# Where the split sums of the dense weights are made, in an attention, mixture and dense-mixture kernel on one core

## The chip, the cores and the metric

The kernel is one program on one core of a Trainium2 chip. The number that counts is the device time of one execution in microseconds; it was run three times, and the median is given. One more execution was recorded by the hardware profiler, and everything that is read from a trace comes from that one.

## The reference

Three stages follow each other. Attention with pooled keys and values gives a matrix x of 4608 tokens by 512. A mixture of 8 experts changes the tokens whose skip score is positive, and a dense layer, called the dense mixture here, ends it.

```python
def reference(**kwargs):
    ...
    x = attention(q, k, v).transpose(0, 2, 1, 3).reshape(4608, 512)
    x = moe(x, w_skip, w_gate, w1, w2)   # one expert of 8 per token:
                                         # x + gate * (relu(x @ w1[e]) @ w2[e])
    h = x @ w_in                         # 512 -> 2048
    return np.maximum(0.01 * h, h) @ w_out   # 2048 -> 512
```

All of it is float32. The kernel gets float32 accuracy out of the matrix engine by splitting each operand into a high and a low half and adding three products: low by high, high by low, high by high.

## The kernel before, in words

**Stages.** Attention runs until about 243 us, the mixture of experts (the first mixture) until about 650 us, the dense mixture from there to the end.

**Engines.** PE is the matrix engine (TensorE), DVE is VectorE, ACT is ScalarE, POOL is GpSimd, and SP issues the transfers. In the first mixture and in the dense mixture PE, DVE, ACT and POOL run in the order in which the program is written. SP's order is set by a scheduler that knows the dependencies.

**The first mixture** takes the experts in the order `TURNS`, in units of at most four tiles of 128 tokens: expert r0 in two units of 4, r6 in one of 2, r1 in two (3 and 2), r7 in one of 1, r2 in two (3 and 2), r3, r4 and r5 in one of 3 each. For a unit, `turn` transposes and splits the gathered tokens, `up` makes one of 8 blocks of the hidden layer, `down` makes one tile of the result and scatters it back to `xd`. An expert has eight loads of raw weights of 512 KB, four of w1 (`split1`) and four of w2 (`split2`): `weight_load` puts one in a buffer `wraw`, `weight_split` makes its high half on ACT (L144) and its low half on DVE (L145), in three rings of pairs. The next expert's w1 is asked for at the last `up` and in the downs of an expert's last unit.

**The dense weights** come as pairs of 32-bit words, 1024 words for 512 values, in 32 halves. `convert` is called in two of eight `up` steps from the second unit on and behind each `down`. It loads one half (`cvraw`), makes two parts of it on ACT (L853, L854), joins them by four operations on DVE (L839 to L842) and adds the rest on POOL (L844) into `cvt`.

Then `finish` takes it on in the first mixture. The up-projection of the dense mixture is a product of 2 by 2 blocks in seven products instead of eight, so it needs four sums of blocks of `w_in`, `ta` and `tb` (DVE, L805 to L808), beside three blocks as they are. Sums and blocks are split (ACT L792, L812, L819; POOL L793, L813, L820) and stored as pairs in `wsd`, the halves of `w_out` in `wod` (L783). The work of one half is spread over four calls of `convert`.

**The dense mixture** takes 768 tokens at a time, six times, in 8 passes p over the hidden layer, so n = 8 s + p runs from 0 to 47. `up2(n)` makes the seven products (42 matmuls, four banks `pu`), puts them together on DVE (`add`, `leaky`) and splits the four results (`pair`: ACT, then POOL). `down2(n)` makes six tiles of 6 matmuls in four banks `pd`, and adds each to `y` (DVE L1213, or on ACT L1211 at p = 0). The program runs `up2(n)` ahead of `down2(n - 1)`. Between the two stand `ws_load(n + 2)`, which loads the pairs of `wsd`, and for p = 3, 4, 5 two `turn_x`, which transpose two tiles of the next 768 tokens into two banks `pd` and copy them on ACT (L1127). The four sums of x that the seven products need (`sums_x`, L1130 to L1133) stand there at p = 6, and its splits (`split_x`, L1137 and L1138) stand between the tiles of the down at p = 7. For the first 768 tokens the turns, sums and splits stand ahead of `up2(0)`.

Of the kernel before, what the change touches and what calls it, by code (L numbers as in the profile page):

```python
# [20 lines left out]
P = 128  # L21
# [9 lines left out]
E = 8  # L31
# [15 lines left out]
RINGS = (4, 4, 3)  # L47
# [7 lines left out]
def kernel(  # L55
# [61 lines left out]
    lst = dram.tile([E * CAP, 1], F32, name="lst")  # L117

# [660 lines left out]
    stages = [[], [], [], []]  # L779
    first_half = {}  # L780

    def pair_out(dst, hi, lo):
        stages[3].append(lambda: (nc.sync.dma_start(out=dst(0), in_=hi.bitcast(F32)), nc.sync.dma_start(out=dst(1), in_=lo.bitcast(F32))))  # L783

    def quarters(t):
        return t.rearrange("p (c q f) -> p q c f", c=2, q=2)

    def finish(cvp, j, h, t, size, low):

        b = j // 2  # L790
        if j % 2:
            nc.scalar.copy(out=low.bitcast(F32R), in_=t)  # L792
            nc.gpsimd.tensor_tensor(out=t.bitcast(F32R), in0=t, in1=low, op=ALU.subtract)  # L793
            pair_out(lambda i: wod[b, :, i, h * 512:(h + 1) * 512], low.bitcast(F32R), t.bitcast(F32R))
            return
        if h == 0:
            first_half[b] = t
            src, m, at = quarters(t)[:, 0:1], 256, 1024
        else:
            src, m, at = quarters(t), 512, 1280  # L800
            q0, q1 = quarters(first_half.pop(b)), src
            ta = cvp.tile([P, 2, 2, P], F32, tag="tf", name=f"ta{b}", bufs=3)
# [4 lines left out]
            V.tensor_tensor(out=ta[:, 1], in0=q1[:, 1], in1=ta[:, 0], op=ALU.subtract)
            V.tensor_tensor(out=tb[:, 1], in0=q1[:, 0], in1=ta[:, 1], op=ALU.subtract)  # L808
            for i, x in enumerate((ta, tb)):
                def sums(i=i, x=x.rearrange("p a c f -> p (a c f)")):  # L810
                    th = cvp.tile([P, 512], F32R, tag="th", name=f"th{b}_{i}", bufs=2)
                    nc.scalar.copy(out=th, in_=x)  # L812
                    nc.gpsimd.tensor_tensor(out=x.bitcast(F32R), in0=x, in1=th.bitcast(F32), op=ALU.subtract)  # L813
                    pair_out(lambda k: wsd[b, :, k, i * 512:(i + 1) * 512], th, x.bitcast(F32R))
                stages[2].append(sums)
        sh = dict(q=m // 256, c=2)
        hi = low[:, :m].bitcast(F32R)
        lo = size[:, :m].bitcast(F32R)
        nc.scalar.copy(out=hi.rearrange("p (q c f) -> p q c f", **sh), in_=src)  # L819
        nc.gpsimd.tensor_tensor(  # L820
            out=lo.rearrange("p (q c f) -> p q c f", **sh), in0=src,
            in1=low[:, :m].rearrange("p (q c f) -> p q c f", **sh), op=ALU.subtract,
        )
        pair_out(lambda i: wsd[b, :, i, at:at + m], hi, lo)

    def convert(cvp):

        for f in [stages[3].pop(0) for _ in range(len(stages[3]))]:
            f()
        for f in [stages[2].pop(0) for _ in range(len(stages[2]))]:  # L830
            f()
        if stages[1]:
            finish(cvp, *stages[1].pop(0))
        if stages[0]:
            j, h, hw, size, low = stages[0].pop(0)
            t = cvp.tile([P, 512], F32, tag="cvt", name=f"cvt{j}_{h}", bufs=3)
# [8 lines left out]
            stages[1].append((j, h, t, size, low))  # L845
        if halves:
# [4 lines left out]
            size = cvp.tile([P, 512], F32, tag="cvs", name=f"cvs{j}_{h}", bufs=4)  # L851
            low = cvp.tile([P, 512], F32, tag="cvl", name=f"cvl{j}_{h}", bufs=4)
# [25 lines left out]
    def ws_load(n):  # L878
        if n < 8 * NSB:
            ws[n] = dense_tiles(rings[1], f"ws{n}", wsd[n % 8], (1024, 768))  # L880

    def wo_load(n):
        if n < 8 * NSB:
            wo[n] = dense_tiles(rings[0], f"wo{n}", wod[n % 8], (1024,))[0]

    with ExitStack() as bctx:
# [4 lines left out]
        state["raws"] = bctx.enter_context(tc.tile_pool(name="raws", bufs=3))  # L891
        NXG = 8
# [97 lines left out]
        for u, (r, t0, n) in enumerate(UNITS):  # L990
# [4 lines left out]
            for f in range(8):  # L995
                up(u, f)
                if last:
                    if f < 4:
                        split2(r, f)
                    elif f == 4:  # L1000
                        ws_load(0)
# [4 lines left out]
                if f == 7 and t0 + n == TILES[r] and not last:  # L1006
                    split1(TURNS[k + 1], 0)
# [3 lines left out]
            if t0 + n == TILES[r] and not last:  # L1011
                todo = [lambda c=c: split1(TURNS[k + 1], c) for c in range(1, 4)]
# [281 lines left out]
```

## Time and profile before

| | us |
|---|---|
| median of three runs (lowest, highest) | 1454.66 (1452.83, 1455.26) |
| the profiled execution | 1452.53 |
| its span in the trace | 1450.7 |
| PE busy | 1345.0 (93% of the span) |
| DVE busy | 994.1 (69%) |
| POOL busy | 529.8 (37%) |
| ACT busy | 465.0 (32%) |

The span runs from the first to the last instruction on the core. The busy time of an engine is the time in which one of its instructions runs. A matmul's time depends on the granted clock, of which a profile gives the mean over a stretch as a share of full speed.

### The profile page before, as it was taken

The page shows a single profiled execution, that of the slowest core. Times are in us where ns is not written, and L with a number is a line of the kernel's source. Part 1 is how long each engine was busy: PE and PEld are TensorE (multiplying, and loading weights), DVE is VectorE, ACT ScalarE, POOL GpSimd, SP SyncE. Part 2 cuts the span into 40 slices and gives each one's busy share as a digit, 9 for nine tenths or more (in the row PEclk, how much of TensorE's full clock was granted, in tenths as well). Part 3 has the DMA queues.
Part 4 walks back from the last instruction along what each step waited for, and adds up shares of the span by engine and source line. Part 5 has one row for each costly group of instructions (what it writes and reads, how often), then busy time and mean ns, then how long its engine had stood idle before and what let it go on. Part 6 is the DMA issues. An engine that isn't in the chain of part 4 may idle for free.

```text
span 1450.7 us, 22090 instructions
## 1 busy us (share of the span) xinstructions
PE 1345.0 (93%) x8296; PEld 1201.4 (83%) x8296; DVE 994.1 (69%) x1647; ACT 465.0 (32%) x800; POOL 529.8 (37%) x458
## 2 busy tenths in 40 slices
PE   4888997998899799996999999999999999999998
PEld 4777886887788689985888988899899989988997
DVE  8676686368898785435668666856766686678565
ACT  2544542353545443323212221222231222213211
POOL 5983002047466372213324332332242233225222
PEclk7899998999897999997999999999999999999999
DMA  9994127357888866564654665556565655547541
GB/s 176 288 286 124 46 79 215 114 188 255 266 275 282 275 220 185 173 239 167 206 208 163 229 210 203 195 197 219 187 215 200 208 192 207 184 160 246 171 156 44
DMA packets 119926, 284.84 MB, mean 196 GB/s; under 512 B 12422, under 2 KB 40070, under 8 KB 119426
## 3 DMA queue, kind: packets, MB, share of 16 engines
q1 hardware_dynamic: 115010, 268.57, 57.5%
q0 software_dynamic: 4800, 14.77, 3.0%
q8 instruction: 67, 1.10, 0.3%
q14 instruction: 49, 0.40, 0.1%
HBM read 234.44 MB, written 49.94 MB: 196 GB/s over the span
## 4 chain that ended last, share of the span: by engine, by line
PE 67%; DVE 13%; DMA 9%; issue 5%; ACT 3%; POOL 2%; SPq 0%; POOLq 0%; DVEq 0%; ACTq 0%
PE d L1207 9%; PE d L1209 8%; PE d L1208 8%; PE u L1154 8%; PE u L1156 8%; PE u L1155 8%; DMA xd<-xg,idx 3%; PE sc L356 2%; DMA cvraw<-in_moe_w_out_dram 2%; PE bank L969 2%; PE pv L407 2%; PE bank L970 2%; PE bank L968 2%; PE bank L952 2%; PE bank L953 2%
## 5 line engine op out<-in xcount | busy, mean ns | idle before, releaser
L1175 POOL TENSOR_TENSOR gl<-g,gh 128x384 fp32r<-128x384 f32 x192 | 210.7, 1107 | 508.2 <-ACT gh L1173 503.8
L1207 PE MATMUL d<-wo_0whi,gl 128*128 128x512 f32 x576 | 226.3, 393 | 12.9 <-DVE y L1213 12.9
L1213 DVE TENSOR_TENSOR y<-d,y 128x512 f32<-128x512 f32 x252 | 168.9, 687 | 91.9 <-PE d L1209 90.8
L1209 PE MATMUL d<-wo_0whi,gh 128*128 128x512 f32 x576 | 225.0, 391 | 0.0
L1208 PE MATMUL d<-wo_0wlo,gh 128*128 128x512 f32 x576 | 224.8, 390 | 0.0
L1173 ACT CAST gh<-g 128x384 fp32r<-128x384 f32 x192 | 98.7, 514 | 307.3 <-DVE g L1169 307.3
L1162 DVE TENSOR_TENSOR g<-u,gp 128x384 f32<-128x384 f32 x144 | 79.8, 554 | 122.4 <-PE u L1156 115.1
L1169 DVE SCALAR_TENSOR_TENSOR g<-g 128x384 f32<-128x384 f32 x192 | 141.2, 735 | 5.0
L1207 PEld LDWEIGHTS d<-wo_0whi,gl 128*128 128x128 f32 x576 | 108.1, 188 | 37.9 <-DVE y L1213 15.0
L1154 PE MATMUL u<-more_h,ws_0wlo 128*128 128x384 f32 x384 | 129.3, 337 | 2.4 <-ACT more_h L1137 1.5
L1155 PE MATMUL u<-more_l,ws_0whi 128*128 128x384 f32 x384 | 129.1, 336 | 1.3 <-DVE more_l L1138 1.3
L1156 PE MATMUL u<-more_h,ws_0whi 128*128 128x384 f32 x384 | 129.0, 336 | 0.0
L953 PE MATMUL bank<-xl,whi 128*128 128x384 f32 (+3 forms) x352 | 120.8, 343 | 7.6 <-DVE xl L942 7.6
L1209 PEld LDWEIGHTS d<-wo_0whi,gh 128*128 128x128 f32 x576 | 108.1, 188 | 23.0
L1208 PEld LDWEIGHTS d<-wo_0wlo,gh 128*128 128x128 f32 x576 | 108.2, 188 | 21.0
L952 PE MATMUL bank<-xh,wlo 128*128 128x384 f32 (+3 forms) x352 | 120.2, 342 | 2.8 <-ACT xh L941 2.7
L954 PE MATMUL bank<-xh,whi 128*128 128x384 f32 (+3 forms) x352 | 120.0, 341 | 0.0
L969 PE MATMUL bank<-wlo,hh 128*128 128x512 f32 x240 | 97.2, 405 | 9.6 <-DVE wlo L145 9.6
L1179 ACT COPY gp<-u 128x384 f32<-128x384 f32 x48 | 23.0, 478 | 258.0 <-PE u L1156 258.0
L976 POOL DMA_INDIRECT xd<-xg,idx x30 | 41.4, 1381 | 171.0 <-DVE xg L972 170.3
L968 PE MATMUL bank<-whi,hl 128*128 128x512 f32 x240 | 97.3, 405 | 5.7 <-ACT whi L144 3.2
L970 PE MATMUL bank<-whi,hh 128*128 128x512 f32 x240 | 96.3, 401 | 0.0
(264 smaller groups left out, 2808.8 us busy)
## 6 DMA issues: line engine op xcount, KB each, us to landing
wraw<-in_moe_w_dram SPq DMA_DIRECT2D x64, 512.0 KB
ws_0whi<-wsd SPq DMA_DIRECT2D x48, 512.0 KB
ws_0wlo<-wsd SPq DMA_DIRECT2D x48, 512.0 KB
wo_0whi<-wod SPq DMA_DIRECT2D x48, 512.0 KB
wo_0wlo<-wod SPq DMA_DIRECT2D x48, 512.0 KB
ws_1whi<-wsd SPq DMA_DIRECT2D x48, 384.0 KB
ws_1wlo<-wsd SPq DMA_DIRECT2D x48, 384.0 KB
xr<-xd SPq DMA_DIRECT2D x36, 256.0 KB
```

The lines of the kernel that those rows point to most:

```text
L952: nc.tensor.matmul(ps, wl[:, c, fs], xh[:, c, :m], start=(c == 0), stop=False)
L953: nc.tensor.matmul(ps, wh[:, c, fs], xl[:, c, :m], start=False, stop=False)
L968: nc.tensor.matmul(ps, hl[:, f, ts_], wh[:, f % 2, :], start=(f == 0), stop=False)
L1154: nc.tensor.matmul(ps, wl[:, c], h[:, c], start=(c == 0), stop=False)
L1155: nc.tensor.matmul(ps, wh[:, c], l[:, c], start=False, stop=False)
L1156: nc.tensor.matmul(ps, wh[:, c], h[:, c], start=False, stop=(c == 1))
L1169: V.scalar_tensor_tensor(out=g[nm], in0=g[nm], scalar=0.01, in1=g[nm], op0=ALU.mult, op1=ALU.max)
L1175: G_.tensor_tensor(out=lo, in0=g[nm], in1=hi.bitcast(F32), op=ALU.subtract)
L1207: nc.tensor.matmul(ps, lo[:, ts_], wh[:, i], start=(i == 0), stop=False)
L1208: nc.tensor.matmul(ps, hi[:, ts_], wl[:, i], start=False, stop=False)
L1209: nc.tensor.matmul(ps, hi[:, ts_], wh[:, i], start=False, stop=(i == 1))
L1213: V.tensor_tensor(out=ys[t], in0=ps, in1=ys[t], op=ALU.add)
```

## The change

`convert` now only converts. Each half, once joined, is stored as it is in a new array `wd` (one store of 256 KB in the place of two pair stores or more), and the sums and splits are made when the dense mixture first needs a block. For n < 8, `ws_load(n)` is `ws_sums(n)` and `ws_blocks(n)`: a load of the whole block `draw` (512 KB), four sums on DVE, their high half on ACT and low half on POOL (1024 columns), and the same for the three blocks (768 columns in two pieces). The pairs are kept in the rings for the pass and stored to `wsd` for the five later ones. `wo_load(n)` does the same for `w_out`, with its low half on DVE. What the first pass loaded in pairs is now loaded once unsplit and stored in pairs. The blocks ws 0, wo 0, wo 1 and the sums of ws 1 are made in the first mixture's last unit, the three blocks of ws 1, wo 2 and wo 3 at the dense start.

Besides: the third ring has four pairs instead of three, the first mixture has a fourth raw buffer and ten gather buffers instead of eight; the raw buffers live through all stages; the next expert's w1 is asked for in the downs of an expert's first unit; in the dense mixture the four sums of x stand one by one behind tiles of the down at p = 6; the splits of x change engines; the six turns ahead of `up2(0)` alternate between ACT and DVE; and for n = 0 the fifth product is issued two places earlier.

In the first mixture this is ACT's row of instructions around the conversion of half 6, in the third unit, before (whi: an expert weight's high half; th, cvl: high halves of dense weights; cvs, cvl at L853 and L854: the conversion's parts; xh: a unit's tokens):

```order
L144 CAST whi_4255<-wraw_4253 128x1024
L812 CAST th_0_4261<-ta_4131 128x512
L812 CAST th_1_4264<-tb_4132 128x512
L792 CAST cvl_0_4058<-cvt_0_4139 128x512
L853 ACTIVATE cvs_0_4276<-cvraw_0_4274 128x512
L854 ACTIVATE cvl_0_4277<-cvraw_0_4274 128x512
L941 CAST xh<-bank_3220 128x4x128
```

And the same place now:

```order
L146 CAST whi_4189<-wraw_4187 128x1024
L807 ACTIVATE cvs_0_4201<-cvraw_0_4199 128x512
L808 ACTIVATE cvl_0_4202<-cvraw_0_4199 128x512
L951 CAST xh<-bank_3226 128x4x128
L951 CAST xh<-bank_3227 128x4x128
```

The three splits of dense weights between the expert weight and the conversion are gone.

On DVE, this is the start of the dense mixture before, up to the first addition of `up2(0)` (xl, more_l: low halves of x and its sums; s: the sums; xf<-tp: a turn's copy; g: an addition):

```order
L1138 TENSOR_TENSOR xl<-xf,xh 128x768
L1127 COPY xf<-tp_4_7838 128x4x128
L1130 TENSOR_TENSOR s_7787<-xf 128x768
L1131 TENSOR_TENSOR s_7788<-s_7787,xf 128x768
L1132 TENSOR_TENSOR xf<-xf 128x2x384
L1133 TENSOR_TENSOR s_7789<-xf,s_7788 128x768
L1138 TENSOR_TENSOR more_l<-s_7788,more_h 128x768
L1138 TENSOR_TENSOR more_l<-xf,more_h 128x768
L1138 TENSOR_TENSOR more_l<-s_7789,more_h 128x768
L1162 TENSOR_TENSOR g_0_7896<-u_0_7889,gp_7887 128x384
```

And now, from the third of its three turn copies:

```order
L1135 COPY xf<-tp_5_7653 128x4x128
L1138 TENSOR_TENSOR s_7600<-xf 128x768
L1139 TENSOR_TENSOR s_7601<-s_7600,xf 128x768
L1147 TENSOR_TENSOR more_l<-xf,more_h 128x768
L1140 TENSOR_TENSOR xf<-xf 128x2x384
L1147 TENSOR_TENSOR more_l<-xf,more_h 128x768
L1141 TENSOR_TENSOR s_7602<-xf,s_7601 128x768
L1147 TENSOR_TENSOR more_l<-s_7602,more_h 128x768
L843 TENSOR_TENSOR wo2wlo<-draw_7685,wo2whi 128x1024
L843 TENSOR_TENSOR wo3wlo<-draw_7693,wo3whi 128x1024
L1171 TENSOR_TENSOR g_0_7717<-u_0_7710,gp_7708 128x384
```

Sums and splits of x are interleaved, and the low halves of two blocks of `w_out` stand ahead of the first addition.

On ACT, this is what stands between `up2(3)` and `up2(4)` before (gp: the first product's copy; gh: high halves of the four results; xf: copies of turns):

```order
L1179 COPY gp_8273<-u_3_8266 128x384
L1173 CAST gh_3_8293<-g_3_8282 128x384
L1173 CAST gh_3_8327<-g_3_8313 128x384
L1173 CAST gh_3_8340<-g_3_8304 128x384
L1173 CAST gh_3_8344<-g_3_8324 128x384
L1127 COPY xf<-tp_0_8356 128x4x128
L1127 COPY xf<-tp_1_8362 128x4x128
L1179 COPY gp_8427<-u_4_8420 128x384
```

And now:

```order
L1182 CAST gh_3_8208<-g_3_8172 128x384
L1182 CAST gh_3_8212<-g_3_8192 128x384
L842 CAST wsT5whi<-tf_8218 128x1024
L842 CAST wsB5whi<-draw_8216 128x256
L842 CAST wsB5whi<-draw_8216 128x512
L1135 COPY xf<-tp_0_8237 128x4x128
L1135 COPY xf<-tp_1_8243 128x4x128
L842 CAST wo6whi<-draw_8297 128x1024
L1188 COPY gp_8312<-u_4_8305 128x384
```

Three high halves of dense weights stand ahead of the two copies of turns, and one behind them.

The diff, cut to its core:

```diff
-RINGS = (4, 4, 3)
+RINGS = (4, 4, 4)
...
+    wd = dram.tile([16, P, 1024], F32, name="wd")
...
-        raw = state["raws"].tile([P, 1024], F32, tag="wraw", name=f"wraw{i}")
+        pool = state["raws2"] if "raws2" in state and i % 4 == 3 else state["raws"]
+        raw = pool.tile([P, 1024], F32, tag="wraw", name=f"wraw{i}")
...
-    stages = [[], [], [], []]
...
-    def pair_out(dst, hi, lo):
-    def finish(cvp, j, h, t, size, low):
...
+    stages = [[], []]
 
     def convert(cvp):
 
-        for f in [stages[3].pop(0) for _ in range(len(stages[3]))]:
-            f()
-        for f in [stages[2].pop(0) for _ in range(len(stages[2]))]:
-            f()
         if stages[1]:
-            finish(cvp, *stages[1].pop(0))
+            j, h, t = stages[1].pop(0)
+            nc.sync.dma_start(out=wd[j, :, h * 512:(h + 1) * 512], in_=t)
...
+    def wd_load(j):
+        raw = state["raws"].tile([P, 1024], F32, tag="wraw", name=f"draw{j}")
+        nc.sync.dma_start(out=raw, in_=wd[j])
+        return raw
+
+    def two_tiles(pool, nm):
+        return [pool.tile([P, 1024], F32R, tag=t, name=f"{nm}{t}") for t in ("whi", "wlo")]
+
+    def pair_of(src, hi, lo, eng):
+        nc.scalar.copy(out=hi, in_=src)
+        eng.tensor_tensor(out=lo, in0=src, in1=hi.bitcast(F32), op=ALU.subtract)
+
+    def keep(dst, at, m, tiles):
+        for i in range(2):
+            nc.sync.dma_start(out=dst[:, i, at:at + m], in_=tiles[i][:, :m].bitcast(F32))
+
+    def ws_sums(n, tfp):
+
+        raw = built[n] = wd_load(2 * n)
+        b = quarters(raw)
+        t = tfp.tile([P, 4, 2, P], F32, tag="tf", name=f"tf{n}")
+        V = nc.vector
+        V.tensor_tensor(out=t[:, 0], in0=b[:, 0, 1], in1=b[:, 0, 0], op=ALU.subtract)
+        V.tensor_tensor(out=t[:, 2], in0=b[:, 1, 1], in1=b[:, 0, 1], op=ALU.subtract)
+        V.tensor_tensor(out=t[:, 1], in0=b[:, 1, 1], in1=t[:, 0], op=ALU.subtract)
+        V.tensor_tensor(out=t[:, 3], in0=b[:, 1, 0], in1=t[:, 1], op=ALU.subtract)
+        tiles = two_tiles(rings[1], f"wsT{n}")
+        pair_of(t.rearrange("p a c f -> p (a c f)"), tiles[0], tiles[1], nc.gpsimd)
+        keep(wsd[n], 0, 1024, tiles)
+        ws[n] = [tiles]
+
+    def ws_blocks(n):
+
+        b = quarters(built.pop(n))
+        tiles = two_tiles(rings[1], f"wsB{n}")
+        hi, lo = (t[:, :768].rearrange("p (q c f) -> p q c f", q=3, c=2) for t in tiles)
+        pair_of(b[:, 0, 0], hi[:, 0], lo[:, 0], nc.gpsimd)
+        pair_of(b[:, 1], hi[:, 1:], lo[:, 1:], nc.gpsimd)
+        keep(wsd[n], 1024, 768, tiles)
+        ws[n].append(tiles)
+
-    def ws_load(n):
-        if n < 8 * NSB:
+    def ws_load(n, tfp):
+        if n < 8:
+            ws_sums(n, tfp)
+            ws_blocks(n)
+        elif n < 8 * NSB:
             ws[n] = dense_tiles(rings[1], f"ws{n}", wsd[n % 8], (1024, 768))
 
     def wo_load(n):
-        if n < 8 * NSB:
+        if n < 8:
+            raw = wd_load(2 * n + 1)
+            wo[n] = two_tiles(rings[0], f"wo{n}")
+            pair_of(raw, *wo[n], nc.vector)
+            keep(wod[n], 0, 1024, wo[n])
+        elif n < 8 * NSB:
...
-                if f == 7 and t0 + n == TILES[r] and not last:
-                    split1(TURNS[k + 1], 0)
...
-            if t0 + n == TILES[r] and not last:
-                todo = [lambda c=c: split1(TURNS[k + 1], c) for c in range(1, 4)]
+            if t0 == 0 and k + 1 < E:
+                todo = [lambda c=c: split1(TURNS[k + 1], c) for c in range(4)]
             if last:
-                todo = [lambda: wo_load(1)]
+                todo = [lambda: wo_load(1), lambda: ws_sums(1, bp1)]
...
-        for t in range(3):
-            turn_x(0, t)
-        split_x(0, V)
-        split_x(1, G_)
-        for t in range(3, NT2):
-            turn_x(0, t, V.tensor_copy if t == 4 else None)
-        ws_load(1)
-        wo_load(2)
-        wo_load(3)
-        sums_x()
-        for i in range(2, 7):
-            split_x(i, (V, G_)[i % 2])
+        for t in range(NT2):
+            turn_x(0, t, V.tensor_copy if t % 2 else None)
+        split_x(0, G_)
+        sums_x[0]()
+        split_x(1, G_)
+        sums_x[1]()
+        split_x(4, V)
+        split_x(2, G_)
+        sums_x[2]()
+        split_x(3, V)
+        sums_x[3]()
+        split_x(5, G_)
+        split_x(6, V)
+        ws_blocks(1)
+        wo_load(2)
+        wo_load(3)
...
-            ws_load(n + 2)
-            if s + 1 < NSB:
+            ws_load(n + 2, c1)
+            if more:
...
-                if p == 6:
-                    sums_x()
...
-                split = []
-                if p == 7 and s + 1 < NSB:
-                    split = [lambda i=i: split_x(i, (V, G_)[i % 2]) for i in range(7)]
-                down2(m, h, split)
+                between = []
+                if p == 6 and more:
+                    between = sums_x
+                if p == 7 and more:
+                    between = [lambda i=i: split_x(i, (G_, V)[i % 2]) for i in range(7)]
+                down2(m, h, between)
```

## Rows read from the trace of the kernel before

**Rows 1.** The page's head.

```profile
span 1450.7 us, 22090 instructions
```

**Rows 2.** Stretches in us: busy by engine (instructions), mean granted clock, DMA share, GB/s.

```profile
336.00:541.00 205.00, 180.03 (x944) 159.41 (x943) 170.69 (x207) 102.08 (x182) 118.00 (x92) 0.88 0.81 265
440.00:469.00 29.00, 28.32 (x138) 26.68 (x137) 23.62 (x31) 14.53 (x29) 20.73 (x15) 0.65 0.88 280
541.00:650.00 109.00, 108.53 (x564) 98.45 (x562) 52.98 (x67) 36.61 (x54) 24.30 (x17) 1.00 0.60 195
650.00:690.00 40.00, 23.90 (x111) 21.25 (x112) 22.04 (x28) 11.57 (x20) 13.10 (x9) 0.79 0.53 183
690.00:1451.00 761.00, 743.96 (x3779) 671.02 (x3777) 518.21 (x803) 177.17 (x334) 242.03 (x202) 1.00 0.55 191
```

The engines stand in the order PE, weight loads of PE, DVE, ACT, POOL.

**Rows 3.** TensorE's waits, 336 to 541: total us, times, longest us.

```profile
PE bank L969 <- DVE wlo L145: 9.6, 6, 4.4
```

**Rows 4.** Timeline of TensorE in the first mixture: start, us, idle before and releaser.

```profile
502.94 0.79 PE L969 MATMUL bank<-wlo,hh 128*128 128x512 f32 x1 [4.39 <-DVE wlo L145]
```

**Rows 5.** ScalarE's waits, 336 to 541.

```profile
ACT cvl L792 <- POOL cvt L844: 29.5, 9, 9.5
ACT cvs L853 <- DMA cvraw<-in_moe_w_out_dram: 26.5, 11, 4.9
...
ACT cvl L819 <- POOL cvt L844: 13.8, 9, 3.5
```

**Rows 6.** VectorE by line, 336 to 541: busy us, mean ns, idle before.

```profile
L145 DVE TENSOR_TENSOR wlo<-wraw,whi 128x1024 fp32r<-128x1024 f32 x30 | 41.4, 1386 | 7.0 <-ACT whi L144 5.4 <-issue 1.5
...
L807 DVE TENSOR_TENSOR ta<-cvt,ta 128x256 f32<-128x256 f32 x6 | 2.5, 412 | 0.0
```

**Rows 7.** Timeline of VectorE and GpSimd from 340.

```profile
340.54 4.84 DVE L840 SCALAR_TENSOR_TENSOR cvt<-cvraw,cvt 128x512 int32<-128x512 int32 x1
341.06 1.31 POOL L813 TENSOR_TENSOR ta<-ta,th 128x512 fp32r<-128x512 f32 x1
```

**Rows 8.** Timeline of SP's queue, the first mixture's start.

```profile
235.10 8.34 SPq L137 DMA_DIRECT2D wraw<-in_moe_w_dram x5
```

**Rows 9.** Timeline of TensorE and VectorE at the dense start.

```profile
661.96 5.42 PE L1126 MATMUL tp<-ident,xr 128*128 128x128 f32 x24 [12.43 <-DMA xr<-xd]
...
673.61 2.56 DVE L1138 TENSOR_TENSOR more_l<-xf,more_h 128x768 fp32r<-128x768 f32 x1
...
678.59 0.55 DVE L1162 TENSOR_TENSOR g<-u,gp 128x384 f32<-128x384 f32 x1
...
689.46 0.39 PE L1207 MATMUL d<-wo_0whi,gl 128*128 128x512 f32 x1
```

**Rows 10.** Timeline around a down at p = 6, the first 768 tokens.

```profile
769.70 0.39 PE L1207 MATMUL d<-wo_0whi,gl 128*128 128x512 f32 x1
...
769.93 0.40 PE L1208 MATMUL d<-wo_0wlo,gh 128*128 128x512 f32 x1
...
771.59 0.56 DVE L1169 SCALAR_TENSOR_TENSOR g<-g 128x384 f32<-128x384 f32 x1
771.71 3.01 POOL L1175 TENSOR_TENSOR gl<-g,gh 128x384 fp32r<-128x384 f32 x2 [1.04 <-ACT gh L1173]
...
772.06 1.78 DVE L1130 TENSOR_TENSOR s<-xf 128x768 f32<-128x768 f32 x1
...
780.98 0.69 DVE L1213 TENSOR_TENSOR y<-d,y 128x512 f32<-128x512 f32 x1 [0.67 <-PE d L1209]
```

**Rows 11.** ScalarE by line, the whole span.

```profile
L144 ACT CAST whi<-wraw 128x1024 fp32r<-128x1024 f32 x64 | 66.1, 1049 | 34.4 <-DMA wraw<-in_moe_w_dram 34.4
...
L1127 ACT COPY xf<-tp 128x512 f32<-128x512 f32 x35 | 18.8, 585 | 30.1 <-DMA xr<-xd 29.5 <-PE tp L1126 0.7
...
L819 ACT CAST cvl<-cvt 128x256 fp32r<-128x256 f32 (+1 forms) x16 | 8.3, 517 | 33.1 <-POOL cvt L844 33.1
```

**Rows 12.** TensorE's waits, 690 to 1451.

```profile
PE d L1207 <- DVE y L1213: 12.9, 5, 2.6
```

More of the change, by code (lines that the diff above doesn't have):

```diff
@@ L844, in convert @@
             nc.gpsimd.tensor_tensor(out=i1, in0=i1, in1=low.bitcast(I32), op=ALU.add)
-            stages[1].append((j, h, t, size, low))
+            stages[1].append((j, h, t))
         if halves:
@@ L850, in convert @@
             w = raw.rearrange("p (n o) -> p n o", o=2)
-            size = cvp.tile([P, 512], F32, tag="cvs", name=f"cvs{j}_{h}", bufs=4)
-            low = cvp.tile([P, 512], F32, tag="cvl", name=f"cvl{j}_{h}", bufs=4)
+            size = cvp.tile([P, 512], F32, tag="cvs", name=f"cvs{j}_{h}")
+            low = cvp.tile([P, 512], F32, tag="cvl", name=f"cvl{j}_{h}")
             nc.scalar.activation(out=size, in_=w[:, :, 1], func=AF.Abs)
@@ L858 @@
     rings = [ctx.enter_context(tc.tile_pool(name=f"ring{i}", bufs=RINGS[i])) for i in range(2)]
+    state["raws"] = ctx.enter_context(tc.tile_pool(name="raws", bufs=3))
     xp = ctx.enter_context(tc.tile_pool(name="xp", bufs=1))
@@ L890 @@
         psb = bctx.enter_context(tc.tile_pool(name="psb", bufs=1, space=PSUM))
-        state["raws"] = bctx.enter_context(tc.tile_pool(name="raws", bufs=3))
-        NXG = 8
+        state["raws2"] = bctx.enter_context(tc.tile_pool(name="raws2", bufs=1))
+        NXG = 10
         xgs = [bp1.tile([P, XW], F32, name=f"xg{i}") for i in range(NXG)]
@@ L1023 @@
             convert(cvp)
+        state.pop("raws2")
     over = nc.values_load(over_i[0:1, 0:1], min_val=0, max_val=1)
@@ L1117, in load_x @@
             for t in range(NT2):
-                xr[s, t] = c6.tile([P, C], F32, tag="xr", name=f"xr{s}_{t}")
+                xr[s, t] = c4.tile([P, C], F32, tag="xr", name=f"xr{s}_{t}")
                 r = s * SB + t * P
@@ L1164, in new @@
             def new(nm):
-                g[nm] = c2.tile([P, HT], F32, tag=f"g{nm}", name=f"g{nm}_{n}")
+                g[nm] = c1.tile([P, HT], F32, tag=f"g{nm}", name=f"g{nm}_{n}")
                 return g[nm]
@@ L1181, in up2 @@
             leaky("11")
+            first = product(4) if n == 0 else None
             add("p", product(2), g["p"])
@@ L1184, in up2 @@
             add("21", product(3), g["p"])
-            add("22", product(4), g["21"])
+            add("22", first or product(4), g["21"])
             g["21"], g["22"] = g["22"], g["21"]
@@ L1237 @@
             s, p = divmod(n, 8)
+            more = s + 1 < NSB
             todo.append((n, up2(n)))
-            ws_load(n + 2)
-            if s + 1 < NSB:
+            ws_load(n + 2, c1)
+            if more:
                 if p == 2:
```

60 lines of the change are left out of this document (12 added, 48 removed).

## The prediction, made before the changed kernel ran

> **What bounds the kernel now.** I read the page's head first: 1450.7 us of span [rows 1]; the profiled execution took 1452.53 us, 2.1 us less than the median of 1454.66, so my sum is made against 1452.5 and gets 2 us at its end. Next the table by stage [rows 2]. The dense stage, 690 to 1451, has TensorE busy for 744 of 761 us at full clock: there, nothing to win but a few waits, and much to lose. The stretch 336 to 541 in the first mixture, where the dense weights are converted, is loose: TensorE is busy for 180.0 of 205 us, and at a granted clock of 0.88, so 25.0 us of idleness and (1 - 0.88) x 180 = 21.6 us of lost clock, 46.6 in all. The third place is the change of stages, 650 to 690, with 23.9 busy of 40.
>
> Who is late in that loose stretch? TensorE's own waits there name VectorE's low half of an expert weight, 9.6 us in 6 waits [rows 3]. Behind such a wait the clock falls: after 4.39 us of it the first matmul took 0.79 us [rows 4] where the same shape takes 0.39 at full clock [rows 10]. VectorE is late because ScalarE is: ScalarE waits 29.5 and 13.8 us for GpSimd's `cvt` before its splits of the dense weights, and 26.5 us for raw weights of `w_out` to land [rows 5]. The expert splits stand behind these in program order.
>
> **What the first mixture gains.** The change removes from `convert` the four sums, both splits and the pair stores. So both of ScalarE's waits for `cvt` go (43.3 us); so do VectorE's four sums of each block (24 in this stretch, the cheapest 0.41 us [rows 6]) and the POOL splits that hold VectorE up: an operation on two inputs, L840, took 4.84 us from 340.54 while POOL's three splits of 1.3 us ran [rows 7]. Stores in this stage fall by my count from 23 to 8.4 MB. An expert's raw weights are also asked for earlier, in the downs of the first unit, with a fourth raw buffer, and that helps the 2-unit experts.
>
> What stays: the one-tile expert r7, 440 to 469, has TensorE busy for 28.3 of 29 us at a clock of 0.65 [rows 2], which loses 0.7 + 9.9 = 10.6 us; four tiles' weights for one tile's work, so I leave that whole. And the waits for raw dense weights (26.5 us and more on ScalarE [rows 5]) keep their cause, SP's queue and the DMA load, though both ease; I leave 6 us for what of them reaches TensorE. 46.6 - 10.6 - 6 = 30 us of gain. Bounds: at least the 9.6 us that TensorE waits for late splits and some 2 us of clock behind them, 12; at most all but the last 6, 40.
>
> **The start of the first mixture.** Before, the first expert load goes at 235.10 [rows 8]; in the new order it stands behind waits for the last attention tiles, as the raw pool is shared. No row prices it. Between 0 (the load was not the last to arrive) and 5, I take +2.
>
> **The last unit of the mixture** gets the sums of two blocks and two `wo` splits. That stretch, 541 to 650, has VectorE busy for 53.0 and POOL for 24.3 of 109 us [rows 2]: that hides them. If the cover were gone they would cost about 2 x 1.39 + 8 x 0.41 = 6 us of VectorE. I put 0 there and 0 at the change of stages.
>
> **The start of the dense stage.** Before, VectorE's first addition of `up2(0)` starts at 678.59, behind its splits of x, of which one took 2.56 us beside POOL; the first down begins at 689.46 [rows 9]. Now VectorE has one x split less, two more copies of turns, and behind the splits the low halves of `wo2` and `wo3`, all ahead of that first addition in program order. The lower bound is 2 x 1.39 [rows 6] + 2 x 0.59 (by ScalarE's copy [rows 11]) less the one split, 3 x 0.41 by its width: 3 us. POOL has four splits of x instead of three, and the block splits B1 (768 columns): two more of 2.56 if they shut VectorE out as the one row shows, so 3 + 5.1 = 8; ScalarE makes three more high halves, 3 x 1.05 [rows 11] = 3.1, ahead of its first copy from `up2(0)`: 11 in all. TensorE can do four products into `pu` and then stops, so all of it is seen. The sums for block 2 stand on VectorE between `up2(0)` and `up2(1)`. Range 3 to 12; I take 11, nearer to the contended row because POOL has five splits of up to 2.56 us, some 13 us, to do in that time.
>
> **The first dense pass, n = 1 to 5.** Each step now makes four sums on VectorE (0.41 each alone [rows 6]), then on ScalarE the high half T (1024 columns, 1.05) and two of B (0.52 each, 1.04 [rows 11]), all between `up2(n)` and the down of n - 1. In the steady state before, with T0 = 769.70 the start of the down, VectorE's last leaky step ends at 772.15 (T0 + 2.45) and POOL's low halves run until 774.72 [rows 10], so the sums end at T0 + 5.4 if the last of them waits for that, and alone at T0 + 4.1. T is done at T0 + 6.5, B at 7.5.
> - n = 3, 4, 5: the copies of the two turns of x stand behind B on ScalarE: the first, 0.59, ends at T0 + 8.1. TensorE wants its bank for the third tile of the down: two turns, eight of the transposes of which 24 took 5.42 us at half clock [rows 9], so 0.9, then two tiles of six matmuls at 0.23 [rows 10], 2.75 together: T0 + 3.6. So it waits 4.5 us, or 3.2 if the sums are alone. 3 x 4.4 = +13 (10 to 14).
> - n = 1: down(0) copies y on ScalarE, behind the same splits: tile 5 is wanted at T0 + 5.5, copied at 8.1; +3.
> - n = 2: y is added on VectorE, right behind the sums: 5.4 + 0.69 [rows 10] against 5.5; +1.
> - Clock after these five waits: a wait of 4.39 us was followed by slow matmuls [rows 4], after 2.6 us there is no stretch below full clock [rows 2]. +4, between 0 and 6.
> The splits of `wo4` to `wo7` come after the down, when `up2` needs VectorE only 2 us later and has four banks: nothing, or about 1 us each if VectorE is late. Nobody waits soon for T's and B's low halves, since the block is used two steps later.
>
> **The later passes.** All TensorE waits after 690 are five, 12.9 us together, for y behind the four sums of x [rows 12]; the sum at 772.06 took 1.78 us [rows 10]. The sums now stand one by one between y additions: -13. Were each sum as long as that one, it would exceed the slack of a tile, 1.38 - 0.69, by 1.1, and 4 us come back; POOL's low halves, which stretched it, are done by then, so I leave this to the range.
>
> **Sum:** 1452.5 + 2 - 30 + 11 + 3 + 1 + 13 + 4 - 13 = 1443.5; with the 2 us to the median, 1445.
>
> **Rivals.**
> - *The raw blocks land late.* In each first-pass step the load of `draw` stands on SP's one queue behind stores that wait for POOL's low halves. If it is late, VectorE's first sum waits, and the next steps' additions with it. The nearest rows are raw dense loads, 26.5 us in 11 waits, 2.4 each and 4.9 at most [rows 5]: 6 x 3.7 = +22, so 1467, slower. It decides from about 2 us a step (12 us bring 1445 to 1457.6). For it: those stores are as many bytes as the loads they replace. Against: the DMA share in the dense stage is 0.55 [rows 2].
> - *The mixture hardly gains.* Raw weights still bound it: SP keeps all 64 expert loads and all raw dense loads, and the DMA share there was 0.81 [rows 2]. Then only the lower bound of 12 comes: 1463.
> - *The mixture is nearly freed*, -40, and the start costs 5: 1445 - 10 - 6 = 1429.
> - *VectorE is shut out by T's low half.* POOL's split of 1024 columns, some 2.6 us (twice the 1.31 of 512 [rows 7]), stands from T0 + 6.5. Where `wo`'s low half or a leaky step has two SBUF inputs and falls into it, it waits to its end: 2.6 us in two or three of the six steps, 5 to 7: 1452. The row of 4.84 us speaks for it; against it, most of VectorE's work then reads PSUM, as y and the additions do.
> The Trainium skill ("SBUF — State Buffer", section "SBUF: two separate sides") says that a VectorE operation with two SBUF inputs and a GpSimd operation that reads SBUF exclude each other for a whole instruction, whoever starts first. By that rule this last case holds in every step where they meet and the start would lie at its upper end; the row of 4.84 us agrees, the 1.78 us of 772.06, shorter than POOL's 3.01 us [rows 10], fits if it slipped in between POOL's two.
>
> **Chances.** Forecast 0.42, with its own range 1437 to 1453 (faster 0.33, same 0.08, slower 0.01); late blocks 0.14 (same 0.01, slower 0.13); small gain 0.14 (same 0.03, slower 0.11); freed 0.20 (all faster); shut out 0.10 (faster 0.04, same 0.04, slower 0.02). A difference of 0.2%, 2.9 us, is about what can be told from none. Faster 0.57, same 0.16, slower 0.27. The range runs from the freed case to the small gain, 1428 to 1464; it leaves out the late blocks' upper half and the ends of the others, some 2 in 10.
>
> **What would show it.** In the profile after: 336 to 541 shorter by 30 and no ScalarE wait on `cvt`; the first down of the dense stage some 11 us later after its stage began; three TensorE waits of about 4 us for ScalarE's copies of x (or y) between n = 1 and 5; no wait for y at p = 6. The forecast is wrong if ScalarE's waits for raw dense weights grow by what the others lose, if VectorE's first sums wait for `draw`, or if TensorE loses clock over the whole first pass.

## The result, and the profile after

The changed kernel took 1438.64 us (median of 4 runs, 1435.5 to 1440.97) against 1453.74 for the kernel before on the same chips: a ratio of 0.9895, 95% interval 0.9872 to 0.9919. The forecast was 1445.

The head of the page of the changed kernel, to be read against [rows 1] and the table ahead of the prediction:

```profile
span 1439.2 us, 21948 instructions
...
PE 1340.5 (93%) x8296; PEld 1193.9 (83%) x8296; DVE 964.2 (67%) x1651; ACT 461.0 (32%) x782; POOL 520.2 (36%) x440
```

The stretches of the changed kernel, with the columns of [rows 2]:

```profile
336.00:541.00 205.00, 195.46 (x1119) 173.74 (x1119) 141.92 (x202) 94.08 (x161) 75.57 (x59) 0.99 0.68 226
...
690.00:1440.00 750.00, 737.55 (x3731) 665.67 (x3729) 521.05 (x813) 182.86 (x339) 267.05 (x216) 0.99 0.56 195
```

The loose stretch in the first mixture is tight now: TensorE has 195.5 busy us of 205 and a clock of 0.99, where it had 180.0 and 0.88. A window of fixed times holds other work in each kernel, however, so the table below cuts each trace at the same matmuls: A from the mixture's first transposes to the first `up` of its second unit, B from there to the end of the last down, C until `up2(0)`, D until the first down of the dense mixture, E until the end of the fifth, F until the end of the last. It is worked out from the starts and ends of TensorE's matmuls in each trace.

| us | A | B | C | D | E | F |
|---|---|---|---|---|---|---|
| before | 53.7 | 351.6 | 17.6 | 22.3 | 73.1 | 684.3 |
| changed | 59.3 | 319.5 | 17.0 | 34.5 | 91.3 | 669.8 |
| e1, x sums spread alone | 55.1 | 349.0 | 17.1 | 22.4 | 73.0 | 669.6 |
| e7, x sums in a row | 56.3 | 319.1 | 16.9 | 36.6 | 89.1 | 687.4 |
| e2, blocks between tiles | 56.6 | 319.1 | 16.7 | 37.5 | 74.5 | 669.9 |
| e4, start in the gap | 56.2 | 317.9 | 17.6 | 30.5 | 91.9 | 669.7 |
| e6, e2 and e4 | 59.5 | 320.3 | 17.0 | 30.3 | 74.9 | 669.9 |
| e5, one step later | 54.0 | 319.5 | 17.3 | 26.2 | 74.3 | 674.3 |
| e10, e6 and block 2 | 56.9 | 320.3 | 18.6 | 25.2 | 81.7 | 670.0 |
| e3, loads as before | 56.1 | 321.3 | 17.6 | 35.8 | 91.1 | 669.9 |
| e8, three stores | 56.4 | 335.6 | 17.3 | 37.2 | 91.4 | 669.9 |
| e9, splits, no stores | 55.4 | 345.6 | 19.1 | 36.3 | 87.9 | 669.9 |
| e11, high halves only | 53.9 | 326.0 | 18.7 | 34.5 | 89.7 | 669.8 |
| e12, low halves only | 53.4 | 347.6 | 18.2 | 36.0 | 91.4 | 669.8 |

B gives 32.1 us, D and E take 12.2 and 18.2, F gives 14.5. F is the spread of the x sums; the rest nets about nothing. TensorE's waits in the changed kernel, 640 to 1440, say where D and E lose:

```profile
PE u L1163 <- ACT gp L1188: 10.5, 2, 5.9
PE d L1217 <- DVE y L1223: 7.8, 4, 2.5
PE d L1217 <- ACT y L1221: 3.3, 1, 3.3
```

None is left at p = 6 ([rows 12] was five of 12.9 us together). Around the down at n = 3, the timeline shows what the first pass does (tf: sums of a block; wsT5whi: their high half; xf: a turn's copy):

```profile
713.27 2.45 POOL L1184 TENSOR_TENSOR gl<-g,gh 128x384 fp32r<-128x384 f32 x2 [1.04 <-ACT gh L1182]
713.63 1.24 DVE L861 TENSOR_TENSOR tf<-draw 128x256 f32<-128x256 f32 x1
...
714.79 1.21 DVE L862 TENSOR_TENSOR tf<-draw 128x256 f32<-128x256 f32 x1
715.93 0.41 DVE L863 TENSOR_TENSOR tf<-draw,tf 128x256 f32<-128x256 f32 x1
...
716.71 1.28 DVE L1223 TENSOR_TENSOR y<-d,y 128x512 f32<-128x512 f32 x2
717.45 0.79 PE L1217 MATMUL d<-wo2whi,gl 128*128 128x512 f32 x1 [2.50 <-DVE y L1223]
718.05 0.63 PE L1218 MATMUL d<-wo2wlo,gh 128*128 128x512 f32 x1
...
718.74 0.58 ACT L1135 COPY xf<-tp 128x512 f32<-128x512 f32 x1
```

Two sums of 0.41 us take 1.24 and 1.21 while POOL's low halves run, the y addition stands behind all four, and TensorE waits 2.50 us for it. Then it runs slow, 0.63 us for a matmul that takes 0.39 at full clock; the granted clock from 718 to 720 is 0.50, the lower of its two levels (1.2 and 2.4 GHz). The copy of the turn, which the prediction named, comes only at 718.74, when TensorE is already at work. At the start of the dense stage:

```profile
640.00 2.33 DVE L1138 TENSOR_TENSOR s<-xf 128x768 f32<-128x768 f32 x1
642.36 2.46 DVE L1139 TENSOR_TENSOR s<-s,xf 128x768 f32<-128x768 f32 x1
...
648.99 2.57 DVE L1141 TENSOR_TENSOR s<-xf,s 128x768 f32<-128x768 f32 x1
...
655.57 0.69 PE L1163 MATMUL u<-more_h,wsT0wlo 128*128 128x384 f32 x1 [5.91 <-ACT gp L1188]
...
669.59 0.69 PE L1163 MATMUL u<-more_h,wsT1wlo 128*128 128x384 f32 x1 [4.63 <-ACT gp L1188]
```

The sums of x are stretched beside POOL's splits, and the first copy of `up2(0)` and of `up2(1)` stands behind the high halves of dense weights.

### The profile page after: what moved, and what is told of

It is laid out like the page before. It is cut to its first block, busy times and chain, and to the rows that moved or that the text cites. A ratio compares the mean times of both kernels' runs of the same rounds, so it can differ in the third digit from the quotient of the medians.

```text
span 1439.2 us, 21948 instructions
## 1 busy us (share of the span) xinstructions
PE 1340.5 (93%) x8296; PEld 1193.9 (83%) x8296; DVE 964.2 (67%) x1651; ACT 461.0 (32%) x782; POOL 520.2 (36%) x440
## 4 chain that ended last, share of the span: by engine, by line
PE 50%; DVE 4%; issue 1%; ACT 0%; POOL 0%; DMA 0%; another core or an unknown queue 0%; SPq 0%; DVEq 0%; ACTq 0%; POOLq 0%
PE d L1217 9%; PE d L1219 9%; PE d L1218 9%; PE u L1165 7%; PE u L1163 7%; PE u L1164 7%; DVE g L1171 1%; PE tp L1134 1%; DVE g L1178 0%; DVE tf L861 0%; DVE tf L862 0%; DMA xr<-xd 0%; DVE y L1223 0%; DVE s L1141 0%; DVE more_l L1147 0%
## 5 line engine op out<-in xcount | busy, mean ns | idle before, releaser
L1217 PE MATMUL d<-wo_0whi,gl 128*128 128x512 f32 x480 | 188.0, 392 | 0.0
L1219 PE MATMUL d<-wo_0whi,gh 128*128 128x512 f32 x480 | 187.4, 390 | 0.0
L1218 PE MATMUL d<-wo_0wlo,gh 128*128 128x512 f32 x480 | 187.2, 390 | 0.0
L1163 PE MATMUL u<-more_h,ws_0wlo 128*128 128x384 f32 x320 | 106.9, 334 | 0.0
L1164 PE MATMUL u<-more_l,ws_0whi 128*128 128x384 f32 x320 | 106.9, 334 | 0.0
L1165 PE MATMUL u<-more_h,ws_0whi 128*128 128x384 f32 x320 | 106.9, 334 | 0.0
L1217 PEld LDWEIGHTS d<-wo_0whi,gl 128*128 128x128 f32 x480 | 90.1, 188 | 19.1 <-ACT xf L1135 0.3
L1219 PEld LDWEIGHTS d<-wo_0whi,gh 128*128 128x128 f32 x480 | 90.1, 188 | 19.1
L1218 PEld LDWEIGHTS d<-wo_0wlo,gh 128*128 128x128 f32 x480 | 90.1, 188 | 17.6
L147 DVE TENSOR_TENSOR wlo<-wraw,whi 128x1024 fp32r<-128x1024 f32 x64 | 83.6, 1316 | 18.5 <-ACT whi L146 18.3
```

Of the source, the lines that this page charges most:

```text
L1163: nc.tensor.matmul(ps, wl[:, c], h[:, c], start=(c == 0), stop=False)
L1164: nc.tensor.matmul(ps, wh[:, c], l[:, c], start=False, stop=False)
L1165: nc.tensor.matmul(ps, wh[:, c], h[:, c], start=False, stop=(c == 1))
L1217: nc.tensor.matmul(ps, lo[:, ts_], wh[:, i], start=(i == 0), stop=False)
L1218: nc.tensor.matmul(ps, hi[:, ts_], wl[:, i], start=False, stop=False)
L1219: nc.tensor.matmul(ps, hi[:, ts_], wh[:, i], start=False, stop=(i == 1))
```

## The experiments

Ratios are to the kernel before on the same chip, with 95% intervals.

**e1: the x sums alone.** The kernel before, with

```diff
-                if p == 6:
-                    sums_x()
...
+                split = sums_x if p == 6 and s + 1 < NSB else []
```

> The kernel before with one part of the change alone: the four sums of x stand one by one behind the first four tiles of the down at p = 6. Theory (the step of the prediction priced at -13): all five waits for y go, so 1453.7 - 13 = 1440 to 1441, which would be the whole net gain of the change. Rival: each sum still delays its tile, and about half comes back: 1447. No wait for y on TensorE by the first, waits of over 1 us at p = 6 by the second.

1438.06 us, ratio 0.9872 (0.9849 to 0.9894), as fast as the whole change. TensorE has no wait at all behind 690, and F is 669.6.

**e7: the change without it.**

```diff
-                if p == 6 and more:
-                    between = sums_x
...
+                if p == 6:
+                    for f in sums_x:
+                        f()
```

> The changed kernel with one part undone: the four sums of x stand in a row ahead of the down at p = 6, as before. Theory (the rest of the change, the sums and splits moved out of the first mixture, nets about nothing): the 14.5 us come back, 1453, the time of the kernel before. Rival (in the changed kernel the waits overlap with others, or the low halves' new engines hide them): 1445.

1455.73 us, ratio 1.0029 (1.0011 to 1.0048). Its waits for y, 690 to 1450:

```profile
PE d L1217 <- DVE y L1223: 20.6, 9, 2.6
```

Less the 7.8 us of the first pass, as in the changed kernel, 12.8 are left for the five p = 6. The two parts of the change add up, and the one in its title, the sums and splits of the weights moved, costs 0.3% by itself.

**e2: the same work between the tiles of the down.** `ws_load` for blocks 3 to 7 becomes a list of four pieces, which `down2` takes up behind tiles 2 to 5:

```diff
-            ws_load(n + 2, c1)
+            if not 1 <= n <= 5:
+                ws_load(n + 2, c1)
...
-                between = []
+                between = ws_pieces(n + 2, c1) if n <= 5 else []
```

> The changed kernel, with the sums and splits of blocks 3 to 7 moved from ahead of the down (and of the turns) to between its tiles: two sums behind tile 2, two behind tile 3, the high and low halves behind tiles 4 and 5. Theory (the five waits in the first pass come only from the place in ScalarE's and VectorE's order): the 5.1 + 0.9 + 12.3 us lost at n = 1 to 5 go but for 1 or 2, so 1438.6 - 17 = 1422. Rival (the work itself, with VectorE and GpSimd shutting each other out, does not fit beside the down): waits for y appear in their place and no more than 5 us are won, 1434.

1423.48 us, ratio 0.9777 (0.9754 to 0.98). E falls from 91.3 to 74.5, where before had 73.1. The waits behind 690:

```profile
PE d L1246 <- ACT xf L1164: 0.3, 1, 0.3
```

The work fits beside the down; its place in the order was nearly the whole loss of E, 16.8 of 18.2 us.

**e4: the start in the gap.**

```diff
-                todo = [lambda: wo_load(1), lambda: ws_sums(1, bp1)]
+                todo = [lambda: wo_load(1)]
...
         load_x(0)
+        ws_sums(1, c1)
+        ws_blocks(1)
+        wo_load(2)
+        wo_load(3)
         for t in range(NT2):
...
         split_x(6, V)
-        ws_blocks(1)
-        wo_load(2)
-        wo_load(3)
```

> The changed kernel, with the sums and blocks of ws 1 and the splits of wo 2 and wo 3 put ahead of the six turns, where all engines wait about 11 us for the rows of x, and none of them in the last unit of the mixture. Theory (they delay the start because they stand behind the splits of x, and T1's low half stands ahead of the last scatter): 1.7 us come from the scatter and 4 from ScalarE's copy and VectorE's first addition, 1438.6 - 6 = 1433. Rival (the start is bound by the splits of x, in which VectorE and GpSimd shut each other out, and the new loads and stores delay the rows of x): 0 to 2 us, 1437.

1434.7 us, ratio 0.9863 (0.9829 to 0.9896); the interval overlaps that of the changed kernel, so the time alone settles nothing. By the stretches D falls by 4.0, as priced, and C does not fall at all (17.0 and 17.6): the 1.7 us of the last scatter were not to be had. D is 34.5 to 37.5 in the eight kernels of the table that have the changed kernel's dense start, with 34.5 the lowest; e4 and e6 (30.5 and 30.3) lie clearly below all of them, but the 4.0 is known to no better than that.

**e6: both together,** the edits of e2 and e4.

> The changed kernel with e2 and e4 together: T1, B1, wo 2 and wo 3 ahead of the turns, blocks 3 to 7 between the tiles of the downs, block 2 still between up2(0) and up2(1). Theory (the two losses are separate places): 15 and 4 us add up, 1438.6 - 19 = 1420. Rival (what the one frees the other uses, GpSimd above all): 1424, as e2 alone.

1418.91 us, ratio 0.9769 (0.9743 to 0.9796): they add up.

**e5: every block one step later**, `ws_pieces(n + 1)` inside the down of n - 1, on top of e6.

```diff
-            if not 1 <= n <= 5:
+            if n > 5:
                 ws_load(n + 2, c1)
...
-                between = ws_pieces(n + 2, c1) if n <= 5 else []
+                between = ws_pieces(n + 1, c1) if n <= 6 else []
```

> The changed kernel, with T1, B1, wo 2 and wo 3 made ahead of the turns and blocks 2 to 7 made one step later, block n + 1 inside the down of n - 1 (blocks first, then the sums), so that nothing of block 2 stands between up2(0) and up2(1). Theory (all that the first pass loses hangs on the place in the engines' order): 1438.6 - 15 (e2) - 4 (the start) - 6 (the 4.6 us wait for ScalarE's copy at up2(1), and its clock) = 1414. Rival (a block that is made only one step ahead is not ready: GpSimd's low half of T ends behind up2's second product): waits for wsT's low half of 1 to 3 us in each of six steps, 1422 to 1428.

1416.33 us, ratio 0.9763 (0.9733 to 0.9794). D falls to 26.2, but F rises by 4.4, and TensorE's waits, 600 to 1420, show why:

```profile
PE u L1192 <- ACT gp L1217: 3.4, 1, 3.4
PE u L1192 <- POOL wsT7wlo L843: 2.5, 1, 2.5
...
PE u L1192 <- POOL wsT3wlo L843: 0.5, 1, 0.5
```

Only the last block, which shares its down with the x sums, is late by 2.5 us, the others by 0.5 at most; the rival held for one step of six. 2.5 of the 4.4 us are this wait, and behind it the granted clock from 756 to 760 was 0.57. By the ratios e5 is not to be told from e6.

**e10: e6, and block 2 in the first down, ahead of block 3.**

```diff
-            if not 1 <= n <= 5:
+            if n > 5:
                 ws_load(n + 2, c1)
...
-                between = ws_pieces(n + 2, c1) if n <= 5 else []
+                between = ws_pieces(2, c1) if n == 1 else []
+                if n <= 5:
+                    between += ws_pieces(n + 2, c1)
```

> e6, with block 2 made between the first tiles of the first down, ahead of block 3, and nothing of it between up2(0) and up2(1). Theory (e5's loss behind its first pass came from blocks made one step late): 4 us less than e6 at up2(1) and nothing given back at p = 6, 1414 to 1415. Rival (two blocks in one down are too much for GpSimd, and up2(2) waits for block 2's low half of T): 1418 to 1420.

1423.11 us, ratio 0.9785 (0.9764 to 0.9806). D is the lowest of all, 25.2, and E rises to 81.7: what was won ahead of the first down is lost behind it. That is worse than either forecast, the rival's 1420 too. The waits, 600 to 1420, hardly name the low half of T that the rival blamed, but ScalarE's first copy again, now in `up2(2)` (2.5 us) where e6 waited 2.6 us for it in `up2(1)`:

```profile
PE u L1192 <- ACT gp L1217: 5.9, 2, 3.4
...
PE u L1192 <- POOL wsT2wlo L843: 0.5, 1, 0.5
```

**e3: the mixture's loads as before.**

```diff
-RINGS = (4, 4, 4)
+RINGS = (4, 4, 3)
...
-        NXG = 10
+        NXG = 8
...
+                if f == 7 and t0 + n == TILES[r] and not last:
+                    split1(TURNS[k + 1], 0)
...
-            if t0 == 0 and k + 1 < E:
-                todo = [lambda c=c: split1(TURNS[k + 1], c) for c in range(4)]
+            if t0 + n == TILES[r] and not last:
+                todo = [lambda c=c: split1(TURNS[k + 1], c) for c in range(1, 4)]
```

> The changed kernel, with the first mixture's loads as they were before: the next expert's w1 asked for in the last unit, three raw buffers, eleven ring pairs, eight gather buffers. The conversion stays without sums and splits. Theory (the gain of 34 us between 336 and 541 comes from ScalarE's waits on the conversion's splits): no more than a quarter is lost, 1438.6 to 1447. Rival (it comes from asking earlier for weights): most of it is lost, 25 us or more, 1464 and above. By the windows, 336 to 541 holds about 195 us of busy TensorE by the first and 185 or less by the second.

1440.02 us, ratio 0.9895 (0.9872 to 0.9919). B is 321.3 against 319.5: asking earlier is worth about 2 of the 32 us, hardly more than B differs among the six kernels above whose mixture stage is that of the changed kernel or nearly so (317.9 to 320.3). The other 30 come from what `convert` no longer does. The theory has the size right; whether ScalarE's waits are the cause, as it says, is another question, and four runs take that apart.

**e8: the bytes without the work.**

```diff
-            nc.sync.dma_start(out=wd[j, :, h * 512:(h + 1) * 512], in_=t)
+            for d in [wd] + more_wd:
+                nc.sync.dma_start(out=d[j, :, h * 512:(h + 1) * 512], in_=t)
```

> The changed kernel, with each converted half stored three times instead of once in the first mixture (two of the stores into arrays that nobody reads), 25 MB instead of 8.4, about the stores of the kernel before. Theory (the gain of some 32 us there comes from the splits and sums that ScalarE, GpSimd and VectorE no longer make): it stays, 1438.6 to 1443. Rival (it comes from the transfers that no longer compete with the loads of weights, and from SP's queue): half of it or more is lost, 1455 or above.

1457.27 us, ratio 1.003 (1.001 to 1.005). B rises by 16.1, half of the gain: the rival's case. Whether it is the bytes or the places that the stores take in SP's queue was not tried. The stretch 336 to 541 has a DMA share of 0.83, about that of before (0.81):

```profile
336.00:541.00 205.00, 187.06 (x1040) 166.07 (x1040) 132.62 (x191) 86.39 (x150) 72.69 (x58) 0.95 0.83 283
```

**e9: the work without the bytes.** `finish` of the kernel before is back, with its stores left out and three of each of its buffers, on top of e3.

```diff
+        for f in [stages[2].pop(0) for _ in range(len(stages[2]))]:
+            f()
         if stages[1]:
-            j, h, t = stages[1].pop(0)
+            j, h, t, size, low = stages[1].pop(0)
             nc.sync.dma_start(out=wd[j, :, h * 512:(h + 1) * 512], in_=t)
+            finish(cvp, j, h, t, size, low)
```

> e3 (the changed kernel with the first mixture's loads as before), with the sums and splits of the kernel before made again in convert, into buffers that nobody stores; the one raw store of each half stays, so the bytes are those of the changed kernel. e8 had the bytes of before without the work and lost 16 of the 32 us between the start of unit 2 and the last down (319.5 to 335.6 us). Theory (work and bytes each hold about half): this stretch goes from e3's 321.3 to about 336, the time to 1455. Rival (work alone finds room when the stores are gone, and the loss is the transfers'): below 327, 1440 to 1445. Third (the work is all of it, and e8's loss another): 348 to 351, 1468.

1466.21 us, ratio 1.0087 (1.0066 to 1.0107). B rises by 24.3 over e3, more than half, and ends between the theory's 336 and the third case's 348. 16 and 24 are more than the 30 that both cost together before: the one hides in part behind the other.

**e11 and e12: which part of the work.** e9 without GpSimd's low halves, and without ScalarE's high halves.

```diff
             nc.scalar.copy(out=low.bitcast(F32R), in_=t)
-            nc.gpsimd.tensor_tensor(out=size.bitcast(F32R), in0=t, in1=low, op=ALU.subtract)
```

(e11; the two other places likewise, and e12 takes away the line above it instead.)

> e9 without the low halves on GpSimd: the four sums and the high halves on ScalarE are still made in the first mixture, and nobody uses them. e9 lost 24 us between the start of unit 2 and the last down (321.3 to 345.6 us). Theory (the work costs because GpSimd's splits stretch VectorE's operations: 26 pieces of each of the three conversion steps take 85 us beside them and 53 without): most of the 24 goes, 325 to 329, time 1442 to 1448. Rival (ScalarE waits for cvt with the expert splits behind it, 57 us of waits in e9): most of it stays, 340 or more, 1460.

> e9 without the high halves on ScalarE: the four sums and GpSimd's operations of the low halves stay (they subtract something else, and nobody uses them). Theory (GpSimd's splits stretch VectorE): most of e9's 24 us stays, 338 to 344, time 1455 to 1462. Rival (ScalarE's waits for cvt): most of it goes, 330 or less, 1450 or less.

e11: 1447.48 us, ratio 0.996 (0.9945 to 0.9975), B up by 4.7 over e3. e12: 1465.15 us, ratio 1.009 (1.0066 to 1.0115), B up by 26.3, beyond the theory's range and as much as e9. So with GpSimd's low halves the loss is there in full, without the high halves too. What the sums and the high halves cost without them is less sure: 4.7 us by B, but the trace is of the fastest of e11's twelve executions (1443.07), and by the ratios e11 is 9 us slower than e3, a third of what e9 and e12 lose (28 us each). ScalarE's waits in e11, 298 to 541, are 37 us for `cvt`, and those 5 to 9 us are the most that they can have cost:

```profile
ACT cvl L812 <- POOL cvt L832: 22.1, 8, 5.8
ACT cvl L789 <- POOL cvt L832: 15.1, 5, 7.0
```

What costs is on VectorE. GpSimd also issues the gathers of tokens, but in e12, 298 to 541, TensorE waits for none of them; it waits for VectorE:

```profile
PE bank L1014 <- DVE wlo L146: 9.9, 5, 4.5
PE bank L998 <- DVE xl L987: 8.6, 3, 3.9
```

The same conversion step, 30 pieces in that stretch, in the kernel before:

```profile
L842 DVE SCALAR_TENSOR_TENSOR cvt<-cvs,cvt 128x512 f32<-128x512 f32 x30 | 38.7, 1290 | 1.2
```

in e11:

```profile
L830 DVE SCALAR_TENSOR_TENSOR cvt<-cvs,cvt 128x512 f32<-128x512 f32 x30 | 20.8, 692 | 1.5 <-ACT xh L984 0.5
```

and in e12:

```profile
L832 DVE SCALAR_TENSOR_TENSOR cvt<-cvs,cvt 128x512 f32<-128x512 f32 x30 | 34.3, 1142 | 1.5 <-DVE cvt L830 0.5
```

692 ns beside little GpSimd work, 1142 to 1290 beside the low halves.

## Why the prediction was right, and where it was not

The sum was made against 1452.5 and came to 1443.5; the profiled execution of the changed kernel took 1440.97. By terms:

- **First mixture, -30: measured -32.1.** Right in size, wrong in cause. The step said that VectorE is late because ScalarE is, and counted ScalarE's 43.3 us of waits for `cvt` [rows 5] first. e11 keeps such waits and loses 4.7 us (9 by the ratios); e12 has none for `cvt` and loses 26.3. What the runs showed is the clause that stood behind it: GpSimd's splits hold VectorE up [rows 7], and beside that the stores (e8), which had no price of their own in the sum. The size was in part luck: the sum left the one-tile expert's 10.6 us whole, but its unit, from its first `up` to the next unit's, takes 21.7 us at a clock of 1.00 where it took 28.1 at 0.64. These 6.4 us came from where nothing was expected, and e12, with the low halves back, has 28.5 at 0.64 again. Nor did the sign that was to refute the forecast do so: ScalarE's waits for raw dense weights, 39.3 us before, did grow by 43, what the others lost. In the changed kernel, 336 to 541, they are

```profile
ACT cvs L807 <- DMA cvraw<-in_moe_w_out_dram: 48.9, 11, 9.6
...
ACT cvs L807 <- DMA cvraw<-in_moe_w_in_dram: 33.4, 8, 9.0
```

and the gain came all the same. As with the waits for `cvt`, the sum of ScalarE's waits did not tell what TensorE paid.

- **Start of the mixture, +2.** 5.6 us in this trace (A), but A is 53.4 to 59.5 among the twelve kernels with the shared raw pool, with 56.2 in the middle, and 53.7 and 55.1 in the two without: +2 fits, and one trace of each would not have told it.
- **Change of stages, 0: -0.6.** The low half of T1 ahead of the last scatter cost nothing that e4 could win back.
- **Dense start, +11: +12.2 (D),** and 12.2 to 15.2 in the eight kernels with this start, so the price was on the low side. e4 shows that some 4.0 of it hang on B1, wo 2 and wo 3 behind the splits of x, e5 that 8.3 go when block 2 is also out of the way of `up2(1)`. The last 3.9 were not tried apart.
- **First pass, +3, +1, +13 and +4: 21 together, +18.2 measured (E).** The step that failed is the third tile's bank. The prediction had it wait 4.4 us for ScalarE's copy of a turn; in the changed program the four banks are dealt out in another order, the third tile gets the bank of the first one and not that of a turn, and it waits for the first y addition, which stands behind the four sums: 2.50, 2.36 and 2.38 us at n = 3, 4 and 5, 7.2 in place of 13. The clock made up for part of it. Each of these waits, and the 3.3 us one at n = 1, was followed by matmuls at half speed. A step lost 4.1 us, 1.7 more than its wait of 2.4; 0.3 of that is lost at full clock too (see the next term), so the clock took some 1.4 us four times, 5 to 6 us in place of the 4 assumed, by this estimate. Errors of opposite sign left the sum nearly right, and that was luck.
- **The later passes, -13: -14.5 (F),** shown by e1 and e7. The waits of [rows 12] are 12.9 us; from the start of one down to that of the next, each of the five steps took 18.4 us before and takes 15.5 now, 0.3 us more than its wait of 2.58.

Of the rivals, the late raw blocks did not come: VectorE waited for `draw` once in the dense stage, 1.7 us. (The 12 us at which they were to decide bring 1445 to 1457, not to 1457.6.) "The mixture hardly gains" is refuted by B. The shut-out by T's low half did not show on TensorE, but the sums were held up by the low halves ahead of it, 1.24 for 0.41. The Trainium skill ("SBUF — State Buffer", section "SBUF: two separate sides") says that a VectorE operation with two SBUF inputs and a GpSimd operation that reads SBUF exclude each other for a whole instruction; the 1.24 us, and the 692 against 1290 ns above, agree.

The changed kernel also has other numbers of buffers than the one before, which the description of the change does not name: one instead of two for the results of `up2`, four instead of six for the rows of x, two instead of three or four for the conversion's `cvt`, `cvs` and `cvl`. In the later passes they cost nothing, as F is 669.6 in e1, with the old numbers, and 669.8 in the changed kernel; for the other stretches no run takes them apart.

## What to carry to other kernels

An engine's waits are not a price. Before one credits a change with the waits that it removes, one asks whether the next engine would have been sooner: here 37 us of ScalarE's waits cost 5 to 9 at most, and a kernel with what GpSimd does to the length of VectorE's instructions, and none of these waits, lost 26. Work moved to where it is first used pays again if it stands in a row at the head of a step; cut into pieces between tiles, it was nearly free (e2, e6). And a change of several parts wants a price for each: the whole net gain here came from a side part, the four sums of x spread over the down.

## What the runs showed of the hardware

TensorE's clock behind waits of nearly the same length differed. In the kernel before, at p = 6:

```profile
777.92 0.50 PE L1207 MATMUL d<-wo_0whi,gl 128*128 128x512 f32 x1 [2.58 <-DVE y L1213]
778.26 0.39 PE L1208 MATMUL d<-wo_0wlo,gh 128*128 128x512 f32 x1
```

and in the changed kernel, at n = 4:

```profile
737.92 0.79 PE L1217 MATMUL d<-wo3whi,gl 128*128 128x512 f32 x1 [2.36 <-DVE y L1223]
738.51 0.63 PE L1218 MATMUL d<-wo3wlo,gh 128*128 128x512 f32 x1
```

Behind the longer wait the engine was at full speed with the second matmul, behind the shorter one the next five took 0.63 us or nearly so. Ahead of the second, but not of the first, stood two turns of transposes. They are not needed for it: e7 has the sums of x in a row, and its five waits at p = 6, of 2.57 or 2.58 us with no turn ahead, had either outcome. Two of these five stretches, with the granted clock as the third number from the end:

```profile
904.70:909.00 4.30, 4.25 (x12) 3.40 (x13) 2.48 (x4) 0.00 (x0) 0.00 (x0) 0.61 0.00 0
1035.80:1040.00 4.20, 4.15 (x20) 3.66 (x21) 3.12 (x5) 0.04 (x1) 0.00 (x0) 1.00 0.07 20
```

The clock fell behind the first two and stayed at full speed behind the last three. So the same wait behind the same work cost the clock in one place and not in another, and in the kernel before in none of five. What decides it stays open.
